# Convolution and gated feed-forward on one core: the band in 32-column tiles behind one scaling, filling matmuls in two places, one step of x last

## The chip, the cores and the metric

The kernel runs on 1 core of one Trainium2 chip. The metric is device microseconds of one execution, and the median over the runs is compared. A core has a matrix engine (TensorE, PE in the profile; its weight loads are PEld), VectorE (DVE), ScalarE (ACT), GpSimd (POOL) and SyncE (SP), which here only issues transfers. Each engine works through its own instructions in order, and they wait for each other by semaphores. Matmuls write to PSUM, and DVE or ACT copies from there to SBUF.

## The reference

A causal convolution over 7 positions, whose 8 heads of 24 channels each have their own softmax weights, followed by a gated feed-forward block:

```python
# x (8, 4096, 192), weight (8, 7)
w = softmax(weight, axis=-1)                      # per head
x_pad = concat([zeros(8, 6, 192), x], axis=1)
conv[b, s, h*24 + g] = sum_k w[h, k] * x_pad[b, s + k, h*24 + g]
t = conv.reshape(32768, 192)
out = (maximum(t @ w_gate, 0) * (t @ w_val)) @ w_out   # 192 -> 1536 -> 192
```

## The kernel before

The 32768 tokens are worked in 16 units of 2 x 1024 tokens (two streams, batches b and b + 4), each unit in two windows of 512. For a window, `gate_val` (L621) multiplies the convolved x, kept with 64 channels of each of two streams on the partitions, by 12 slices of the gate and value weights; ACT applies the relu (L632), DVE multiplies (L633), and `project_turn` (L643) multiplies by the output weights. For most of the run the convolution for later units is done beside this by ACT, DVE and POOL.

The first window has nothing to work beside, so its convolution is done by TensorE, in a prologue with this order:

1. Seven matmuls on constants (L193, `hold`, by the counts in `WARM`, in units of 128 columns) keep TensorE occupied. They write to the first bank of a PSUM tile called `held`. Four stand ahead of the spreading matmul (L203), which copies the 8 x 7 weights to 128 partitions as soon as their transfer lands, and three behind it.
2. DVE and ACT make the softmax (L275 to L295). Three DVE instructions (L299) scale the 22-wide row of weights and mask it by head, for heads 0 to 2, 3 to 5 and 6 to 7. The result is `blocks`, 128 x 8 x 22.
3. Three matmuls with zeros (L209) clear three PSUM areas. The third area is the second bank of `held`. Then 8 matmuls for each area (L335) place `blocks` along a diagonal, 16 rows at a time, so that a 118 x 112 band matrix stands there for each head. DVE casts the three areas to f16, `bands` (L343).
4. `conv_steps` (L391) multiplies x by the bands. The window is cut into 5 steps of up to 106 positions and the 192 channels into 3 groups c of 64. A step of a group is 8 matmuls, four at a time in four column tiles. Group 0 needs the first band only, group 1 also the second, group 2 the second and third. x comes from f32 rows that ACT casts step by step (L119) in the order `STEPS0 = [1, 0, 2, 3, 4]`; step 4 has its own transfer, which lands last. The order is: group 0 steps 1, 0, 2; group 1 steps 1, 0; group 0 steps 3, 4; group 1 steps 2, 3, 4; then group 2.
5. `evict` (L402) casts each group from PSUM to the f16 tile `dense[0]`, 512 columns at once: group 0 on ACT, 1 on DVE, 2 on ACT. DVE also copies the first slices of the gate and value weights to the upper partitions (`both_halves`, L231).
6. The first gate and value matmuls (L621) go by groups: gate and value of group 0, then of group 1, then of group 2, four matmuls each, which run in two pairs.

The order on each engine is that in which the code is written. Semaphore waits are set by the tile framework from what each instruction reads and writes.

Of the kernel before, what the change touches and what calls it, by code (L numbers as in the profile page):

```python
# [15 lines left out]
def kernel(  # L16
# [27 lines left out]
    STEPS = [6, 5, 2]  # L44
    TAPS = [(6, 5), (4, 3), (2, 1, 0)]
    GSUB = 5
    WARM = [(4, 4, 4, 1), (4, 4, 1)]
    STEPS0 = [1, 0, 2, 3, 4]
    CONV1 = 10


# [242 lines left out]
    nc.vector.tensor_reduce(out=blk[:, 0, :], in_=prod[:], axis=mybir.AxisListType.X, op=ALU.add)  # L294
    nc.vector.reciprocal(sm[:], sm[:])  # L295
    blocks = const.tile([128, H, BW], F16)
    for heads in BANDS:
        n = len(heads)
        nc.vector.scalar_tensor_tensor(  # L299
            out=blocks[:, heads[0] : heads[0] + n, :],  # L300
            in0=blk[:].to_broadcast([128, n, BW]),
            scalar=sm[:],
            in1=mask[:, heads[0] : heads[0] + n, :].to_broadcast([128, n, BW]),
            op0=ALU.mult,
            op1=ALU.mult,
        )
    wn = const.tile([128, KW], FP)
    nc.gpsimd.tensor_scalar(
        out=wn[:], in0=e[:, 0:KW], scalar1=sm[:], scalar2=None, op0=ALU.mult
# [18 lines left out]
    for part, heads, to, copy in zip(  # L328
        raised, BANDS, bands, [nc.vector.tensor_copy] * 3
    ):  # L330
        n = len(heads)
        for j in range(128 // HR):
            s0 = HR * j - PAD
            lo, hi = max(0, -s0), min(BW, SUB - s0)
            nc.tensor.matmul(  # L335
                out=part[:, 0 : SUB * n].rearrange("p (h t) -> p h t", t=SUB)[:, :, s0 + lo : s0 + hi],
                lhsT=Z[:, 112 - HR * j : 240 - HR * j],
                rhs=blocks[:, heads[0] : heads[0] + n, lo:hi],
                start=False,
                stop=(j == 128 // HR - 1),  # L340
                skip_group_check=True,
            )
        copy(out=to[:].rearrange("p h t -> p (h t)"), in_=part[:, 0 : SUB * n])  # L343

    tap = const.tile([128, NCH, KW], FP)

# [30 lines left out]
    def conv_steps(g, ps, c, steps):  # L377


        for jj in steps:  # L380
            col = STEP * jj
            n = min(STEP, WIN - col)
            rows = n + PAD
            for second in range(2):
                for st in range(2):
                    for k2 in range(2):
                        k = 2 * c + k2
                        h0, h1 = 32 * k // G, (32 * k + 31) // G
                        h, m = (h0, G * h1 - 32 * k) if second else (h1, 32)
                        p0 = 64 * st + 32 * k2  # L390
                        nc.tensor.matmul(  # L391
                            out=ps[p0 : p0 + m, 0, col : col + n],
                            lhsT=xts[g][0:rows, jj, st, 32 * k : 32 * k + m],
                            rhs=band(h)[0:rows, 0:n],
                            start=True,
                            stop=True,
                            tile_position=(0, p0),
                            skip_group_check=True,
                        )

    def evict(copy, g, ps, c):
        copy(out=dense[0][:, g, c, :], in_=ps[:, 0, :])  # L402

    def conv(g):

# [301 lines left out]

    dense[0] = xcpool.tile([128, 2, NCH, WIN], F16, name="xc")
    first = [psum.tile([128, 2, 512], FP, name="ps") for _ in range(NCH)]
    for c, steps in ((0, STEPS0[:3]), (1, STEPS0[:2]), (0, STEPS0[3:]), (1, STEPS0[2:]), (2, STEPS0)):  # L710
        conv_steps(0, first[c], c, steps)
    both_halves(nc.vector.tensor_copy, 0, Wg)
    both_halves(nc.vector.tensor_copy, 0, Wv)
    for c, copy in enumerate((nc.scalar.copy, nc.vector.tensor_copy, nc.scalar.copy)):
        evict(copy, 0, first[c], c)
    both_halves(nc.vector.tensor_copy, 1, Wg)
    both_halves(nc.vector.tensor_copy, 1, Wv)
    xts[2] = load_x(2)
# [82 lines left out]
```

## Time and profile before

| | |
|---|---|
| median of 3 runs (lowest, highest) | 761.65 us (761.57, 763.04) |
| span of the profiled execution, first to last instruction | 760.2 us |
| median less span | 1.45 us |
| TensorE busy | 756.0 us, 99% of the span |
| spreading matmul (L203) starts | 2.76 us |
| first band matmul (L335) starts | 4.97 us |
| first convolution matmul (L391) starts | 6.12 us |
| first gate matmul on groups 0, 1, 2 (L621) starts | 7.81, 8.24, 8.70 us |
| last matmul starts | 757.0 us |

Times within an execution are microseconds from the start of its span. A row of the timeline gives start, length, engine, line of the kernel, operation, tile written <- tile read, shape and count; in brackets stand the idle time of the engine just before it and what ended that. Rows of equal instructions are merged, so the length of a merged row reaches from the first start to the last end. Ends of matmuls are modelled.

### The profile page before, as it was taken

The page shows a single profiled execution, that of the slowest core. Times are in us where ns is not written, and L with a number is a line of the kernel's source. Part 1 is how long each engine was busy: PE and PEld are TensorE (multiplying, and loading weights), DVE is VectorE, ACT ScalarE, POOL GpSimd, SP SyncE. Part 2 cuts the span into 40 slices and gives each one's busy share as a digit, 9 for nine tenths or more (in the row PEclk, how much of TensorE's full clock was granted, in tenths as well). Part 3 has the DMA queues.
Part 4 walks back from the last instruction along what each step waited for, and adds up shares of the span by engine and source line. Part 5 has one row for each costly group of instructions (what it writes and reads, how often), then busy time and mean ns, then how long its engine had stood idle before and what let it go on. Part 6 is the DMA issues. An engine that isn't in the chain of part 4 may idle for free.

```text
span 760.2 us, 30531 instructions
## 1 busy us (share of the span) xinstructions
PE 756.0 (99%) x13724; PEld 454.8 (60%) x13724; DVE 675.8 (89%) x647; ACT 610.1 (80%) x680; POOL 461.3 (61%) x311
## 2 busy tenths in 40 slices
PE   9999999999999999999999999999999999999998
PEld 5555555565565666656666565666656556566658
DVE  7889989998998989989999899998999989897891
ACT  7897887878878788887877878788797887877671
POOL 8729649195591946829377392874919659193600
PEclk9999999999999999999999999999999999999999
DMA  8953532345324443333434324352243531240302
GB/s 142 137 69 92 79 85 46 43 96 75 85 44 52 97 66 85 55 61 83 60 85 71 66 67 55 85 85 69 56 49 93 77 86 44 23 100 9 85 2 85
DMA packets 153714, 54.07 MB, mean 71 GB/s; under 512 B 148912, under 2 KB 153584, under 8 KB 153584
## 3 DMA queue, kind: packets, MB, share of 16 engines
q1 hardware_dynamic: 117376, 37.78, 21.6%
q0 software_dynamic: 35808, 14.07, 16.4%
q8 instruction: 107, 1.75, 1.0%
q10 hardware_dynamic: 400, 0.27, 0.1%
q14 instruction: 23, 0.19, 0.1%
HBM read 28.98 MB, written 25.17 MB: 71 GB/s over the span
## 4 chain that ended last, share of the span: by engine, by line
PE 99%; DMA 0%; ACT 0%; issue 0%
PE ps L621 65%; PE ps L643 31%; PE ps L686 2%; PE ps L391 0%; DMA w<-in_weight_dram 0%; PE ps L193 0%; PE ps L335 0%; PE ps L414 0%; PE ps L209 0%; PE ps L203 0%; ACT out_s L697 0%; ACT L127 0%
## 5 line engine op out<-in xcount | busy, mean ns | idle before, releaser
L633 DVE TENSOR_TENSOR hT<-gr,ps 128x1024 f16<-128x1024 f16 (+1 forms) x385 | 469.1, 1219 | 35.5 <-ACT gr L632 8.7
L632 ACT ACTIVATE gr<-ps 128x1024 f16<-128x1024 f32 (+1 forms) x385 | 392.8, 1021 | 114.4 <-PE ps L621 114.4
L550 POOL TENSOR_TENSOR prod<-prod,prod 128x896 f32<-128x896 f32 x145 | 302.6, 2087 | 251.8 <-DVE prod L584 242.7
L621 PE MATMUL ps<-xc,Wg 64*64 64x512 f16 (+1 forms) x4464 | 318.4, 376 | 0.0
L621 PE MATMUL ps<-xc,Wv 64*64 64x512 f16 (+1 forms) x4464 | 318.3, 376 | 0.0
L643 PE MATMUL ps<-hT,Wo 64*64 64x512 f16 x4320 | 235.8, 376 | 0.0
L621 PEld LDWEIGHTS <-Wv 64*64 64x64 f16 (+1 forms) x4464 | 149.9, 106 | 98.5 <-DVE hT L633 0.3
L621 PEld LDWEIGHTS <-Wg 64*64 64x64 f16 (+1 forms) x4464 | 145.4, 107 | 103.4 <-issue 0.2
L643 PEld LDWEIGHTS <-Wo 64*64 64x64 f16 x4320 | 137.3, 107 | 95.7
L538 ACT ACTIVATE prod<-x_r,tap 128x1024 f32<-128x1024 f16 (+2 forms) x195 | 182.7, 1017 | 0.0
L574 DVE SCALAR_TENSOR_TENSOR acc<-x_r,tap,acc 128x1024 f32<-128x1024 f16 (+3 forms) x150 | 118.0, 854 | 0.0
L661 DVE STREAM_TRANSPOSE out_s<-ps 128x1024 f32<-128x1024 f32 x45 | 56.2, 1248 | 28.4 <-PE ps L643 24.4
L550 POOL TENSOR_TENSOR xc<-prod,prod 128x896 f16<-128x896 f32 x29 | 60.6, 2089 | 2.3
L479 POOL COPY x_p<-x_e 128x1536 f16<-128x1536 f16 (+1 forms) x32 | 42.2, 1351 | 0.0
L251 POOL DMA_DIRECT2D x_e<-in_x_dram x30 | 26.6, 890 | 0.0
L574 DVE SCALAR_TENSOR_TENSOR xc<-x_r,tap,acc 128x1024 f16<-128x1024 f16 (+3 forms) x30 | 25.2, 840 | 0.0
L563 ACT ACTIVATE acc<-x_r,tap 128x1024 f32<-128x1024 f16 (+3 forms) x30 | 22.5, 800 | 0.0
L656 ACT COPY turned_by<-ps 128x2 f32<-128x2 f32 x45 | 7.0, 155 | 16.8 <-PE ps L643 14.8
L686 PEld LDWEIGHTS <-hT 128*128 128x128 f16 x192 | 15.8, 98 | 0.4 <-issue 0.4
L686 PE MATMUL ps<-Wo,hT 128*128 128x192 f16 x192 | 16.0, 246 | 0.0
L697 ACT COPY out_s<-ps 128x768 f32<-128x768 f32 (+2 forms) x5 | 3.2, 638 | 12.7 <-PE ps L686 12.7
L697 DVE COPY out_s<-ps 128x192 f32<-128x192 f32 x1 | 0.4, 359 | 13.3 <-PE ps L686 13.3
(61 smaller groups left out, 74.4 us busy)
## 6 DMA issues: line engine op xcount, KB each, us to landing
out_dram<-out_s SPq DMA_DIRECT2D x125, 192.0 KB
x_e<-in_x_dram POOLq DMA_DIRECT2D x28, 384.0 KB, 6.3
x_r<-x_p SPq DMA_TRANSPOSE x116
prod<-in_moe_w_out_dram POOLq DMA_DIRECT2D x1, 576.0 KB, 8.7
prod<-in_x_dram SPq DMA_DIRECT2D x3, 168.0 KB
out_dram<-out_s SPq DMA_DIRECT2D x5, 96.0 KB
out_s<-in_x_dram POOLq DMA_DIRECT2D x2, 210.0 KB, 6.2
out_s<-in_x_dram POOLq DMA_DIRECT2D x2, 192.0 KB, 6.1
```

Of the source, the lines that this page charges most:

```text
L251: nc.gpsimd.dma_start(out=xe[:, 0:n, st, :, :].rearrange("p j c r -> p j (c r)"), in_=bass.AP(tensor=x.tensor, offset=x.offset + row * D, ...
L479: nc.gpsimd.tensor_copy(out=xp[:, js, :, st, :], in_=xe[:, js, st, :, :])
L538: nc.scalar.activation(out=both(prods[b, k], b, at, n), in_=shifted(b, c, k, t, n), func=ACTF.Copy, scale=tap[:, c, k : k + 1],)
L550: nc.gpsimd.tensor_tensor(out=acc if k < KW - 1 else xcs[b][:, w, :, :].rearrange("p c t -> p (c t)")[:, LDVE : NCH * WIN], in0=acc, in1=p ...
L563: nc.scalar.activation(out=both(accs[b], b, at, n), in_=shifted(b, c, 0, t, n), func=ACTF.Copy, scale=tap[:, c, 0:1],)
L574: nc.vector.scalar_tensor_tensor(out=result(b, at, n) if k == KW - 1 else both(acc, b, at, n), in0=shifted(b, c, k, t, n), scalar=tap[:, c ...
L621: nc.tensor.matmul(out=pss[i][q : q + M, st, :], lhsT=W[64 * st : 64 * st + 64, c, 128 * f + q : 128 * f + q + M], rhs=xcb[64 * st : 64 * ...
L632: nc.scalar.activation(out=gr[:, sts], in_=pss[0][:, sts], func=ACTF.Relu)
L633: nc.vector.tensor_tensor(out=h[:, f, sts], in0=gr[:, sts], in1=pss[1][:, sts], op=ALU.mult)
L643: nc.tensor.matmul(out=ps[64 * st : 64 * st + 64, b, :], lhsT=Wo[64 * r : 64 * r + 64, f, p, :], rhs=hs[b][64 * r : 64 * r + 64, f, st, :] ...
L661: nc.vector.transpose(out=o[:].rearrange("p t (b d) -> p b t d", b=2)[:, :, :, 32 * p : 32 * p + 32], in_=ps[:].rearrange("p b (t c) -> p ...
L686: nc.tensor.matmul(out=ps[:, i // 2, D * (i % 2) : D * (i % 2) + D], lhsT=h[:, f, st, 128 * q : 128 * (q + 1)], rhs=Wo[:, f, :, :].rearran ...
```

## The change

- The burst ahead of the spreading matmul is 4, 4, 4, 3 units of 128 columns instead of 4, 4, 4, 1.
- `blocks` is made by one DVE instruction over all 8 heads instead of three.
- The band matmuls write 32 partitions instead of 128, each in a column tile of its own (`tile_position=(0, q)`), in the order `PLACED`, so that four neighbours in the order have four different tiles.
- Two filling matmuls of 512 and 256 columns (`hold(*WARM[2])`) stand between the band and the first convolution. They write to the first bank of `held`, whose second bank held the third area of the band.
- The convolution's order is group 0 steps 1, 0, 2, 3; group 1 the same; then step 4 of group 0 and of group 1; then group 2.
- Groups 0 and 1 are copied out in two pieces: columns 0 to 317 (steps 0 to 2) and 318 to 511 (steps 3 and 4). Group 0's first piece is on DVE, ahead of the copies of the weights, and its second on ACT; group 1's first is on ACT and its second on DVE.

```diff
-    WARM = [(4, 4, 4, 1), (4, 4, 1)]
+    WARM = [(4, 4, 4, 3), (4, 4, 1), (4, 2)]
     STEPS0 = [1, 0, 2, 3, 4]
+    PLACED = [0, 2, 4, 6, 1, 3, 5, 7]
...
-    for heads in BANDS:
-        n = len(heads)
-        nc.vector.scalar_tensor_tensor(
-            out=blocks[:, heads[0] : heads[0] + n, :],
-            in0=blk[:].to_broadcast([128, n, BW]),
-            scalar=sm[:],
-            in1=mask[:, heads[0] : heads[0] + n, :].to_broadcast([128, n, BW]),
-            op0=ALU.mult,
-            op1=ALU.mult,
-        )
+    nc.vector.scalar_tensor_tensor(
+        out=blocks[:],
+        in0=blk[:].to_broadcast([128, H, BW]),
+        scalar=sm[:],
+        in1=mask[:].to_broadcast([128, H, BW]),
+        op0=ALU.mult,
+        op1=ALU.mult,
+    )
...
-        for j in range(128 // HR):
+        for j in PLACED:
+            q = HR * j // 32 * 32
             s0 = HR * j - PAD
             lo, hi = max(0, -s0), min(BW, SUB - s0)
             nc.tensor.matmul(
-                out=part[:, 0 : SUB * n].rearrange("p (h t) -> p h t", t=SUB)[:, :, s0 + lo : s0 + hi],
-                lhsT=Z[:, 112 - HR * j : 240 - HR * j],
+                out=part[q : q + 32, 0 : SUB * n].rearrange("p (h t) -> p h t", t=SUB)[
+                    :, :, s0 + lo : s0 + hi
+                ],
+                lhsT=Z[:, 112 - HR * j + q : 144 - HR * j + q],
                 rhs=blocks[:, heads[0] : heads[0] + n, lo:hi],
                 start=False,
-                stop=(j == 128 // HR - 1),
+                stop=(j % 2 == 1),
+                tile_position=(0, q),
                 skip_group_check=True,
             )
         copy(out=to[:].rearrange("p h t -> p (h t)"), in_=part[:, 0 : SUB * n])
+    hold(*WARM[2])
...
-    def evict(copy, g, ps, c):
-        copy(out=dense[0][:, g, c, :], in_=ps[:, 0, :])
+    def evict(copy, g, ps, c, cols=slice(0, WIN)):
+        copy(out=dense[0][:, g, c, cols], in_=ps[:, 0, cols])
...
-    for c, steps in ((0, STEPS0[:3]), (1, STEPS0[:2]), (0, STEPS0[3:]), (1, STEPS0[2:]), (2, STEPS0)):
+    for c, steps in ((0, STEPS0[:4]), (1, STEPS0[:4]), (0, STEPS0[4:]), (1, STEPS0[4:]), (2, STEPS0)):
         conv_steps(0, first[c], c, steps)
+    early_cols, late_cols = slice(0, 3 * STEP), slice(3 * STEP, WIN)
+    evict(nc.vector.tensor_copy, 0, first[0], 0, early_cols)
     both_halves(nc.vector.tensor_copy, 0, Wg)
     both_halves(nc.vector.tensor_copy, 0, Wv)
-    for c, copy in enumerate((nc.scalar.copy, nc.vector.tensor_copy, nc.scalar.copy)):
-        evict(copy, 0, first[c], c)
+    evict(nc.scalar.copy, 0, first[0], 0, late_cols)
+    evict(nc.scalar.copy, 0, first[1], 1, early_cols)
+    evict(nc.vector.tensor_copy, 0, first[1], 1, late_cols)
+    evict(nc.scalar.copy, 0, first[2], 2)
```

Where this puts the instructions is shown at two places, with the semaphores that each instruction waits for (DVE_49 counts what DVE has finished, PE_49 what TensorE, Activation_49 what ACT). The line numbers of the changed kernel are a few higher: L193 became L194, L343 L346, L391 L395, L402 L406 and L621 L625.

The first place is TensorE between the band matmuls and the convolution. Before, with the first matmul of each channel group (`band_188`, `band_189` and `band_190` are the first, second and third band; x is in `out_s`):

```order
L335 MATMUL ps<-blocks,Z 128x2x6
L391 LDWEIGHTS out_s [waits Activation_49]
L391 MATMUL ps<-band_188,out_s 32x106 [waits DVE_49]
...
L391 MATMUL ps<-band_189,out_s 32x106 [waits DVE_49]
...
L391 MATMUL ps<-band_190,out_s 32x106 [waits DVE_49]
```

The same place now; the three bands are `band_186`, `band_187` and `band_188`:

```order
L335 MATMUL ps<-blocks,Z 32x2x6
L194 LDWEIGHTS const-bfloat16-1.0
L194 MATMUL ps<-const-bfloat16-1.0 128x512 [waits DVE_49]
L194 LDWEIGHTS const-bfloat16-1.0
L194 MATMUL ps<-const-bfloat16-1.0 128x256
L395 LDWEIGHTS out_s [waits Activation_49]
L395 MATMUL ps<-band_186,out_s 32x106
...
L395 MATMUL ps<-band_187,out_s 32x106 [waits PE_49]
...
L395 MATMUL ps<-band_188,out_s 32x106 [waits PE_49]
```

The waits of the three first readers for DVE, which casts the bands, are gone. The first filling matmul, ahead of them all, has the only wait for DVE.

The second place is where the groups are copied out (`xc` is the tile `dense[0]`). Before, on ACT and then on DVE from the third band cast on:

```order
L119 CAST out_s<-prod_90 96x384 [waits DMAHW4_49]
L402 CAST xc<-ps 128x512 [waits PE_49] x2
...
L343 CAST band_190<-ps 128x224 [waits PE_49]
L231 COPY Wg<-Wg 64x3x128 [waits DMASW0_49]
L231 COPY Wv<-Wv 64x3x128 [waits DMASW1_49]
L402 CAST xc<-ps 128x512 [waits PE_49]
```

The same now, ACT first:

```order
L120 CAST out_s<-prod_90 96x384 [waits DMAHW4_49]
L406 CAST xc<-ps 128x194 [waits DVE_49]
L406 CAST xc<-ps 128x318 [waits PE_49]
L406 CAST xc<-ps 128x512 [waits PE_49]
...
L346 CAST band_188<-ps 128x224 [waits PE_49]
L406 CAST xc<-ps 128x318 [waits PE_49]
L232 COPY Wg<-Wg 64x3x128 [waits DMASW0_49]
L232 COPY Wv<-Wv 64x3x128 [waits DMASW1_49]
L406 CAST xc<-ps 128x194 [waits Activation_49]
```

ACT's piece of group 0 waits for DVE and no longer for TensorE, and DVE's piece of group 1 waits for ACT. The copies of the two weight slices now stand behind DVE's piece of group 0.

## The prediction

> **What bounds the kernel now.** I read the page first: its first part and the shares of the chain that ended last.
>
> ```profile
> span 760.2 us, 30531 instructions
> PE 756.0 (99%) x13724; PEld 454.8 (60%) x13724; DVE 675.8 (89%) x647; ACT 610.1 (80%) x680; POOL 461.3 (61%) x311
> PE ps L621 65%; PE ps L643 31%; PE ps L686 2%; PE ps L391 0%; DMA w<-in_weight_dram 0%; PE ps L193 0%; PE ps L335 0%; PE ps L414 0%; PE ps L209 0%; PE ps L203 0%; ACT out_s L697 0%; ACT L127 0%
> ```
>
> TensorE (PE) is busy for 99% of the span and is the chain itself. From the gate and value matmuls (L621) on, nothing else holds it, so whatever moves their start moves the end by as much. The change lies wholly ahead of them. So I read the chain of waits for the first 12 us (start, length, what):
>
> ```profile
> 0.87 1.75 DMA w<-in_weight_dram
> 2.76 0.56 PE ps L203 x2
> 3.32 1.07 PE ps L193 x3
> 4.39 0.75 PE ps L209 x3
> 5.14 1.05 PE ps L335 x24
> 6.19 1.61 PE ps L391 x120
> 7.81 4.33 PE ps L621 x37
> ```
>
> This chain says PE throughout, but pieces of PE here are themselves held by VectorE (DVE) and ScalarE (ACT). The timeline of the same stretch shows by whom (start, length, engine, line; the last columns are the idle time before and its releaser):
>
> ```profile
> 4.06 1.78 ACT L119 CAST out_s<-prod 112x384 f16<-112x384 f32 x4
> 4.63 0.67 DVE L299 SCALAR_TENSOR_TENSOR blocks<-blk,sm,mask 128x66 f16<-128x66 f32 x3
> 4.97 1.22 PE L335 MATMUL ps<-blocks,Z 128*128 128x48 f16 x24
> 5.56 0.51 DVE L343 CAST band<-ps 128x336 f16<-128x336 f32 x1 [0.26 <-PE ps L335]
> 5.56 1.22 DVE L343 CAST band<-ps 128x336 f16<-128x336 f32 x3 [0.26 <-PE ps L335]
> 5.99 0.50 DVE L343 CAST band<-ps 128x336 f16<-128x336 f32 x1
> 6.12 1.68 PE L391 MATMUL ps<-band,out_s 112*32 112x106 f16 x120
> 6.18 0.51 ACT L119 CAST out_s<-prod 96x384 f16<-96x384 f32 x1 [0.34 <-DMA prod<-in_x_dram]
> 7.17 0.58 ACT L402 CAST xc<-ps 128x512 f16<-128x512 f32 x1 [0.48 <-PE ps L391]
> 7.81 0.39 PE L621 MATMUL ps<-xc,Wg 64*128 64x512 f16 x2
> 8.06 0.58 ACT L402 CAST xc<-ps 128x512 f16<-128x512 f32 x1 [0.30 <-PE ps L391]
> 8.24 0.40 PE L621 MATMUL ps<-xc,Wg 64*128 64x512 f16 x2
> 8.45 0.40 PE L621 MATMUL ps<-xc,Wv 64*128 64x512 f16 x2
> 8.70 0.39 PE L621 MATMUL ps<-xc,Wg 64*128 64x512 f16 x2
> ```
>
> The convolution starts at 6.12, 0.05 after the first band cast ends (5.56 + 0.51 = 6.07). The first gate matmul starts at 7.81, 0.05 after channel group 0 is copied out (7.17 + 0.58). Groups 1 and 2 are first read at 8.24 and 8.70, which are the marks to beat. A hand-over from one engine to another costs about 0.05.
>
> Two paces of PE follow. The 24 band matmuls stream 154 columns for each of 8 heads, 1232 in 1.05 us: 0.85 ns a column. A pair of 512 columns takes 8.45 - 8.24 = 0.21: 0.41 ns a column. The convolution is already at the fast pace: its second group can start at 5.99 + 0.50 + 0.05 = 6.54, and its last 96 matmuls, 24 rounds of four, start by 6.12 + 1.68 - 0.21 = 7.59 (0.21 is the length of one, quoted below), 0.045 a round, or 0.42 a column. So PE doubles its pace at about 6.1, after 2.8 us of work without a pause since 3.32.
>
> **The change part by part.** Durations for the new shapes come from these groups (count, busy, mean ns):
>
> ```profile
> L391 PE MATMUL ps<-band,out_s 112*32 112x106 f16 x48 | 1.6, 212 | 0.0
> L574 DVE SCALAR_TENSOR_TENSOR acc<-x_r,tap,acc 128x1024 f32<-128x1024 f16 x70 | 89.1, 1272 | 0.0
> L574 DVE SCALAR_TENSOR_TENSOR acc<-x_r,tap,acc 128x256 f32<-128x256 f16 x70 | 33.6, 479 | 0.0
> L299 DVE SCALAR_TENSOR_TENSOR blocks<-blk,sm,mask 128x66 f16<-128x66 f32 x2 | 0.5, 292 | 0.0
> L343 DVE CAST band<-ps 128x336 f16<-128x336 f32 x2 | 0.9, 502 | 0.3 <-PE ps L335 0.3
> L697 DVE COPY out_s<-ps 128x192 f32<-128x192 f32 x1 | 0.4, 359 | 13.3 <-PE ps L686 13.3
> L697 ACT COPY out_s<-ps 128x384 f32<-128x384 f32 x1 | 0.5, 478 | 1.2 <-PE ps L686 1.2
> L697 ACT COPY out_s<-ps 128x192 f32<-128x192 f32 x1 | 0.3, 318 | 1.5 <-PE ps L686 1.5
> ```
>
> *Filling ahead of the spreading matmul.* 256 columns more, 0.22 us at 0.85. The burst it joins is over long before the weight lands (0.87 + 1.75 = 2.62). Cost: nothing; without that cover, 0.22.
>
> *One scaling of all heads.* The first of three pieces took 0.29 and let the band start at 4.97. One piece of 176 columns takes 0.292 + 110 x 1.03 ns (slope of the L574 rows) = 0.41 and ends at 5.04; the band starts at 5.09, 0.12 later.
>
> *Band in 32-column tiles.* No row shows such a tile at the slow pace. The nearest is the convolution, in which four column tiles run at once. Two rounds of 66 columns cost 0.11 for each set of heads, where eight matmuls of 462 columns in all took 0.39. From the first matmul to the first cast was 5.56 - 4.97 = 0.59, so 0.20 of it is not streaming; now 0.31, and the first cast starts at 5.40. If the tiles did not overlap it would stay 0.59: 5.68. I take 5.40. The three casts still follow each other on DVE for 1.22, so the third ends at 6.62 instead of 6.78 (bound 6.90).
>
> *Filling matmuls ahead of the convolution.* Here the rows of the order decide. Before, the first reader of each band waited for DVE by itself; now none does, and the first filling matmul has the only wait for DVE between band and convolution. It must therefore stand for all three casts. PE works in order, so the convolution, which used to start after the first cast, now stands behind the third: the filling starts at 6.62 + 0.05 = 6.67. Its 768 columns cost 0.32 at the fast pace and 0.65 at the slow one. I take the slow one: the pace changed after 2.8 us of unbroken work, and now PE has stood still from about 5.4 to 6.67, so the filling is the first work after a pause. For the convolution I take the fast pace, the only one that it shows. Call its start P = 7.32 (6.99 with fast filling). Loss so far 1.20.
>
> *Step 4 of x last, and the split copies.* Nothing is left to gain from the order of steps: the cast of step 4 is over at 6.18 + 0.51 = 6.69, before P. Group 0 is finished after 64 + 8 matmuls, 18 rounds, P + 0.81. Before, it was finished 8 rounds after 6.54, at 6.90, and read at 7.17, so 0.28 lies between. DVE starts the early piece at P + 1.09. It cannot start sooner: the ACT piece of step 4 waits for DVE alone, so DVE's piece must already stand behind step 4. The early piece, 318 columns, takes 0.48 (502 less 18 x 1.0); ACT's late piece starts 0.04 after its end and takes 0.32; the first gate matmul follows at P + 1.09 + 0.48 + 0.04 + 0.32 + 0.05 = P + 1.98. One copy of 0.58 has become two in a row. The copies of Wg and Wv stand behind the early piece on DVE, and at 0.4 and 0.3 us they are done by P + 2.1, beside ACT's piece.
>
> Group 1: ACT goes on about 0.08 before its last piece ends (four casts of 0.505 in 1.78), takes 318 columns in 0.42 (318 + 126 x 0.83, slope of the ACT rows) until P + 2.27; DVE's piece waits for ACT, 0.04 + 0.36, so PE reads group 1 at P + 2.72. Group 2: ACT follows at P + 2.2 and is done at P + 2.8, ahead of its reader 0.43 after group 1 (two pairs). Nothing to pay there; before, 0.46 lay between, so 0.03 comes back.
>
> **Sum.** Group 1 is read at 7.32 + 2.72 = 10.04 against 8.24: 1.80 later, less 0.03: **+1.77 us** on the profiled span of 760.2. What lies around the span (761.65 - 760.2 = 1.45) I leave as it is, so the median 761.65 becomes **763.4**. Nothing later gives it back: PE is full from there on.
>
> **The rivals.** *Fast filling* (0.23): PE is at its fast pace at 6.67, P = 6.99, +1.44, 763.1. For it: PE is as busy from 3.32 to 5.4 as before. Against it: the pause.
>
> *Slow convolution* (0.20): the pause keeps PE slow until group 0 is done; 18 rounds of 106 x 0.85 = 0.09 instead of 0.045 add 0.81, +2.58, 764.2. For it: a burst with a pause behind it, the one up to 3.32, did not bring the fast pace. Against it: no slow row of the convolution. [...]
>
> *Only one of the two waits costs* (0.11): filling free of the third cast, copies in a row: P = 6.06, group 1 at 8.78, +0.51; or filling held, pieces side by side: group 0 at P + 0.81 + 0.28 + 0.32 + 0.05 = 8.78, group 2 at P + 2.43 = 9.75 (conv's end P + 1.35, 0.44 to ACT as now, 0.58, 0.05), +1.05. Between 762.2 and 762.7.
>
> *The change does what it says* (0.06), not slower: the filling waits for the first band at most and lies in the time of its cast, from the band's end at 5.41 to 6.06 (slow pace); the pieces leave as steps end. P = 6.06, group 2 at P + 2.43 = 8.49 against 8.70: -0.21, 761.4. It holds if the third cast ends after the filling starts; the order speaks against it.
>
> **How the numbers follow.** The forecast has 0.40. About 0.2% (1.52 us, 763.17) is what a measurement of this kernel can tell from no change. Slower by more: most of the forecast (0.34), a little under half of fast filling (0.11), all of slow convolution (0.20): 0.65. Within: the rest of these, both cases of one wait, and most of the last: 0.32. Faster: 0.03, since the whole head before 7.81 offers no such gain. The range 762.6 to 764.6 holds the forecast, fast filling, most of the slow convolution and a part of the one-wait case; 0.3 either way around 763.4 is the likeliest's own.
>
> **What would show it.** In the new timeline: the first band cast at about 5.4 and the third's end near 6.6; PE idle from 5.4 to 6.7; the filling (L194) starting only behind the third cast (L346), two matmuls over 0.65 or 0.32; the convolution (L395) as one block from about 7.3; on ACT the piece of 194 columns starting only when DVE's 318 end; the first gate matmul (L625) at 9.3, group 1 at 10.0. Wrong if the filling starts before 6, if DVE's early piece starts before step 4 is done, or if the convolution runs in rounds of 0.09.

## The result, and the profile after

The changed kernel is slower: a median of 764.77 us (763.48 to 768.26, 7 runs) against 762.53 us (761.57 to 763.04, 7 runs) for the kernel before, a ratio of 1.0037 with a 95% interval of 1.0022 to 1.0051. That is 0.17 above the forecast's range and 1.4 above its time. The spread grew too: 1.5 us before, 4.8 now.

The execution that was profiled is the quickest of the seven (763.48, span 761.8), and has to be read as such. Its page, first part and the first line of the shares of the chain that ended last:

```profile
span 761.8 us, 30535 instructions
...
PE 756.0 (99%) x13726; PEld 425.8 (56%) x13726; DVE 677.1 (89%) x646; ACT 610.8 (80%) x681; POOL 461.3 (61%) x311
...
PE 99%; DVE 1%; ACT 0%; issue 0%
```

TensorE has as much to do as before (756.0), and the span is 1.6 longer. New in the chain is 1% of DVE. The chain of waits shows where it stands (start, length, what; its rows from 4.89 on):

```profile
4.89 0.27 PE ps L335 x8
5.18 1.23 DVE band L346 x3
6.46 0.49 PE ps L194 x2
6.94 1.08 PE ps L395 x80
8.05 0.49 DVE xc L406
8.57 0.55 DVE Wg L232
9.11 0.46 DVE Wv L232
9.62 4.47 PE ps L625 x36
```

Before, the chain was PE alone from 2.76 on. Now it leaves TensorE twice in these rows: for the three band casts in a row, and for DVE's early piece with two weight copies behind it. (Ahead of them, from 3.14 to 4.89, it runs through the softmax and the scaling on DVE and ACT.) The timeline of the same stretch (start, length, engine, line, operation; last the idle time before and its releaser):

```profile
4.43 0.40 DVE L298 SCALAR_TENSOR_TENSOR blocks<-blk,sm,mask 128x176 f16<-128x176 f32 x1
...
4.89 0.35 PE L335 MATMUL ps<-blocks,Z 128*32 128x48 f16 x24
5.18 1.22 DVE L346 CAST band<-ps 128x336 f16<-128x336 f32 x3 [0.35 <-PE ps L335]
...
6.46 0.49 PE L194 MATMUL ps<-const-bfloat16-1.0 128*128 128x512 bf16 x2 [1.22 <-DVE band L346]
...
6.87 1.57 PE L395 MATMUL ps<-band,out_s 112*32 112x106 f16 x120
...
8.05 0.49 DVE L406 CAST xc<-ps 128x318 f16<-128x318 f32 x1 [1.64 <-PE ps L395]
...
8.47 0.50 POOL L232 COPY Wg<-Wg 64x384 f16<-64x384 f16 x1
8.57 0.55 DVE L232 COPY Wg<-Wg 64x384 f16<-64x384 f16 x1
...
8.94 0.62 PE L625 MATMUL ps<-xc,Wg 64*128 64x512 f16 x2 [0.50 <-ACT xc L406]
9.04 0.52 DVE L232 COPY Wv<-Wv 64x384 f16<-64x384 f16 x1
...
9.59 0.36 DVE L406 CAST xc<-ps 128x194 f16<-128x194 f32 x1
...
9.99 0.91 DVE L232 COPY Wg<-Wg 64x384 f16<-64x384 f16 x1
10.01 0.39 PE L625 MATMUL ps<-xc,Wg 64*128 64x512 f16 x2
...
10.44 0.40 PE L625 MATMUL ps<-xc,Wg 64*128 64x512 f16 x2
...
10.87 0.38 PE L625 MATMUL ps<-xc,Wg 64*128 64x512 f16 x1
```

The 24 band matmuls are done in 0.35 instead of 1.22 (0.48 at the slow pace, in the next profile), and most of what they won is lost at once: TensorE then stands still for 1.22, until the third cast is done and the filling can start. Groups 0, 1 and 2 are read at 8.94, 10.01 and 10.44, against 7.81, 8.24 and 8.70. The last group is 1.74 later, as forecast, in an execution that is not the typical one.

The changed kernel run again (`again`, median 765.2) was profiled in an execution of 765.07, close to its median. Its timeline, TensorE alone:

```profile
4.89 0.48 PE L335 MATMUL ps<-blocks,Z 128*32 128x48 f16 x24
6.51 0.80 PE L194 MATMUL ps<-const-bfloat16-1.0 128*128 128x512 bf16 x2 [1.14 <-DVE band L346]
7.24 2.75 PE L395 MATMUL ps<-band,out_s 112*32 112x106 f16 x120
9.94 0.61 PE L625 MATMUL ps<-xc,Wg 64*128 64x512 f16 x2
...
10.74 0.66 PE L625 MATMUL ps<-xc,Wg 64*128 64x512 f16 x2
...
11.60 0.66 PE L625 MATMUL ps<-xc,Wg 64*128 64x512 f16 x2
12.02 0.61 PE L625 MATMUL ps<-xc,Wv 64*128 64x512 f16 x2
12.45 0.83 PE L625 MATMUL ps<-xc,Wg 64*128 64x512 f16 x6
```

Same program, same order, and all of it at half the pace until 12.45: the convolution in 2.75 instead of 1.57, the gate pairs 0.43 apart instead of 0.22. The row at 12.45 is the seventh pair. Before, the seventh pair stood at 9.13:

```profile
8.91 0.39 PE L621 MATMUL ps<-xc,Wv 64*128 64x512 f16 x2
9.13 0.83 PE L621 MATMUL ps<-xc,Wg 64*128 64x512 f16 x6
```

So 12.45 - 9.13 = 3.32 is lost by the seventh pair, against 3.1 in the span (763.3 - 760.2). In the quick execution the seventh pair stands at 10.87, 1.74 later than before. The other 1.58 comes with the slow pace, in the same order of instructions, and it is the difference of the two times (765.07 - 763.48 = 1.59).

### The profile page after: what moved, and what is told of

Same layout as the page of the kernel before. It is cut to its first block, busy times and chain, and to the rows that moved or that the text cites. A ratio compares the mean times of both kernels' runs of the same rounds, so it can differ in the third digit from the quotient of the medians.

```text
span 761.8 us, 30535 instructions
## 1 busy us (share of the span) xinstructions
PE 756.0 (99%) x13726; PEld 425.8 (56%) x13726; DVE 677.1 (89%) x646; ACT 610.8 (80%) x681; POOL 461.3 (61%) x311
## 4 chain that ended last, share of the span: by engine, by line
PE 99%; DVE 1%; ACT 0%; issue 0%
PE ps L625 65%; PE ps L647 31%; PE ps L690 2%; PE ps L395 0%; PE ps L194 0%; DVE band L346 0%; PE ps L418 0%; DVE Wg L232 0%; PE ps L204 0%; DVE xc L406 0%; DVE Wv L232 0%; DVE blocks L298 0%; DVE prod L288 0%; ACT out_s L701 0%; DVE blk L295 0%
## 5 line engine op out<-in xcount | busy, mean ns | idle before, releaser
L625 PE MATMUL ps<-xc,Wg 64*64 64x512 f16 (+1 forms) x4464 | 314.8, 376 | 0.5 <-ACT xc L406 0.5
L625 PE MATMUL ps<-xc,Wv 64*64 64x512 f16 (+1 forms) x4464 | 314.9, 376 | 0.1
L625 PEld LDWEIGHTS <-Wv 64*64 64x64 f16 (+1 forms) x4464 | 143.9, 106 | 105.0 <-DVE Wv L232 0.4
L625 PEld LDWEIGHTS <-Wg 64*64 64x64 f16 (+1 forms) x4464 | 134.4, 107 | 115.1 <-DVE Wg L232 0.9
L647 PEld LDWEIGHTS <-Wo 64*64 64x64 f16 x4320 | 126.3, 107 | 106.7
```

Of the source, the lines that this page charges most:

```text
L625: nc.tensor.matmul(out=pss[i][q : q + M, st, :], lhsT=W[64 * st : 64 * st + 64, c, 128 * f + q : 128 * f + q + M], rhs=xcb[64 * st : 64 * ...
L647: nc.tensor.matmul(out=ps[64 * st : 64 * st + 64, b, :], lhsT=Wo[64 * r : 64 * r + 64, f, p, :], rhs=hs[b][64 * r : 64 * r + 64, f, st, :] ...
```

## The experiments

Each kernel ran in five rounds beside the kernel before, whose median was 762.56, 762.41, 762.60 and 762.76 in the four groups. Since the distributions have long upper ends, the table has three numbers for each: the median less that of before, the lowest time, and how many executions lay above 764.2 (2 of 134 did for the kernel before). "Waits" says whether the filling stands behind the third band cast, "pieces" whether groups 0 and 1 leave in two pieces.

| kernel | waits | pieces | median less before | lowest | above 764.2 |
|---|---|---|---|---|---|
| changed kernel (the runs of the result) | yes | yes | +2.24 | 763.48 | 6 of 7 |
| again | yes | yes | +2.64 | 763.46 | 11 of 12 |
| wideband | yes | yes | +2.54 | 763.45 | 6 of 10 |
| weightsfirst | yes | yes | +2.69 | 763.22 | 5 of 7 |
| slicesfirst | yes | yes | +1.65 | 763.26 | 6 of 11 |
| wholecopy | yes | no | +2.51 | 762.67 | 4 of 6 |
| fillonly | yes | no | +0.74 | 762.43 | 5 of 12 |
| keepbusy | yes, pause filled | yes | +1.37 | 763.47 | 4 of 11 |
| keepbusy_slices | yes, pause filled | yes | +1.10 | 763.38 | 4 of 11 |
| keepbusy_whole | yes, pause filled | no | +0.56 | 762.69 | 1 of 11 |
| fillspread | no | yes | +0.94 | 762.61 | 1 of 11 |
| fillspread_whole | no | no | +0.41 | 761.96 | 2 of 11 |
| nofill | no filling | yes | +0.49 | 762.03 | 2 of 11 |
| nofill_whole | no filling | no | +0.39 | 762.10 | 0 of 11 |
| splitonly | no filling | yes | -0.06 | 762.13 | 0 of 11 |
| warmonly | no filling | no | -0.05 | 761.87 | 0 of 11 |
| poolslice | no filling | no | -0.22 | 761.90 | 0 of 11 |

None of these kernels leaves out a part of the computation: the filling matmuls compute nothing that the output needs.

### The wait of the filling

**again**: the changed kernel, nothing edited.

> The changed kernel unaltered, for a second profile in another phase of the clock. In the first profile TensorE was at its fast pace already at 4.9 us (band matmuls), the span was 761.8, and the run was the fastest of seven (763.48, median 764.77). Theory 'pause': in the slower executions TensorE is at the slow pace for some part of 5 to 11 us, and this profile, if its span is 763 or more, shows filling matmuls 0.43 apart, convolution rounds of 0.09 or gate pairs of 0.43 there. Rival 'elsewhere': the slower executions lose their 1 to 2 us after 11 us, and the first 11 us look like the first profile's.

Measured: 765.2 (763.46 to 769.85), ratio 1.0039 (1.0026 to 1.0053). The profile is shown above. The forecast's time is that of its quickest executions, and its typical one is slow through the convolution and the first gate pairs.

**nofill** takes the two filling matmuls away:

```diff
-    hold(*WARM[2])
```

> Leaves out only the two filling matmuls ahead of the convolution. Theory 'wait': the convolution starts 0.05 after the first band cast, at about 5.74 instead of 6.87, group 1 is read at about 8.45 (10.01 in the changed kernel, 8.24 before), and the median comes back to within 0.5 us of the kernel before. Rival 'copies': the loss lies in the copies in two pieces; the median stays 1.5 us or more above the kernel before.

Measured: 763.05, ratio 1.0008 (0.9999 to 1.0016). Its timeline, TensorE alone:

```profile
5.13 0.48 PE L335 MATMUL ps<-blocks,Z 128*32 128x48 f16 x24
6.05 1.80 PE L394 MATMUL ps<-band,out_s 112*32 112x106 f16 x120 [0.43 <-DVE band L346]
8.30 0.39 PE L624 MATMUL ps<-xc,Wg 64*128 64x512 f16 x2 [0.45 <-ACT xc L405]
```

The convolution stands behind the first cast alone again, 0.43 after the band. Without the two matmuls 2.15 of the 2.64 are gone, so the median came out as the theory of the wait had it. The marks inside did not: the convolution starts at 6.05 (expected 5.74), group 1 is read at 9.02 (expected 8.45).

**fillspread** keeps both matmuls and lets them write to a bank that no cast reads:

```diff
-                out=held[:, 0, 0 : 128 * reps],
+                out=(held[:, 0, :] if at is None else at)[:, 0 : 128 * reps],
...
-    hold(*WARM[2])
+    hold(*WARM[2], at=spread[:, 1, :])
```

> The same two filling matmuls, written to the second bank of the PSUM tile of the spreading matmul, which DVE and ACT have long read. Theory 'wait': it is the wait for the third cast that costs, not the 768 columns; the filling runs at about 5.1, the convolution starts at 5.4 to 5.8, and the median is that of the kernel without filling, to 0.4 us. Rival 'columns': the filling itself is on the path and the median stays 0.6 us or more above the kernel without filling.

Measured: 763.5, ratio 1.0006 (0.9998 to 1.0015). So the wait, with what follows from it, costs 1.7 (765.2 - 763.5). The columns of the filling cost 0.45 by the medians (763.5 - 763.05), between the two expectations, and nothing by the ratios (1.0006 here, 1.0008 in nofill), so a price for them is not shown. What makes the wait is the tile `held` that filling and third area share: the two are in different banks and never overlap.

### The pause and the pace

**keepbusy** keeps the wait and gives TensorE 1536 more columns, which wait for nothing, ahead of the filling that waits:

```diff
+    hold(4, 4, 4, at=spread[:, 1, :])
     hold(*WARM[2])
```

> The changed kernel with three more filling matmuls of 512 columns, written to the spreading matmul's tile, between the band and the filling that waits: TensorE works through most of its pause of 1.4 us, and the convolution still starts behind the third cast. Theory 'pause': the pause makes TensorE fall back to or stay at the slow pace in most executions, so the median falls from 764.8 to about 763.5 and the spread of the runs narrows to about 1 us. Rival 'phase': the spread comes from when the clock rises at all, whatever TensorE does; median and spread stay as in the changed kernel.

Measured: 763.93, ratio 1.0021 (1.0009 to 1.0032). The pause shrinks from 1.14 to 0.45, the convolution starts at 6.87 as in the changed kernel's quick profile, and the median falls by 1.27 although TensorE was given more to do. Work without a purpose made the kernel faster, so about half of the loss in the median goes with the pause and not with the wait itself. The spread did not narrow to 1 us as expected: the times reach from 763.47 to 768.36, and four of 11 still lay above 764.2.

**fillonly** is the kernel before with the waiting filling alone:

```diff
-    WARM = [(4, 4, 4, 1), (4, 4, 1)]
+    WARM = [(4, 4, 4, 1), (4, 4, 1), (4, 2)]
...
+    hold(*WARM[2])
```

> The kernel before with nothing but the two filling matmuls of 512 and 256 columns ahead of the convolution, in the tile of the third band. Theory 'wait': the filling starts 0.05 after the third cast, near 6.83, the convolution at 7.15 (fast pace) or 7.48 (slow) instead of 6.12; the median is 1.0 to 1.7 us above the kernel before. The band takes 1.05 here, so TensorE's pause is 0.8 and not 1.4, and the slowest runs should stay below those of the changed kernel. Rival: filling between band and convolution is hidden, median within 0.4 us.

Measured: 763.34, ratio 1.0016 (1.0007 to 1.0025): 0.74 above the kernel before, under the 1.0 to 1.7 expected. Behind the old, long band the pause is 0.64 in the profile, and five of 12 executions lay above 764.2.

**wideband** is the changed kernel with the band in 128 columns, one matmul after the other, as before:

```diff
-                out=part[q : q + 32, 0 : SUB * n].rearrange("p (h t) -> p h t", t=SUB)[
+                out=part[:, 0 : SUB * n].rearrange("p (h t) -> p h t", t=SUB)[
...
-                lhsT=Z[:, 112 - HR * j + q : 144 - HR * j + q],
+                lhsT=Z[:, 112 - HR * j : 240 - HR * j],
...
-                tile_position=(0, q),
```

> The changed kernel with one part undone: the band matmuls write all 128 columns again, one after the other, about 1.05 us instead of 0.35, all else as changed. TensorE's pause ahead of the filling becomes about 0.65 instead of 1.2 to 1.4. Theory A (the length of the pause decides when the fast pace comes): the median falls though TensorE has more to do, to 763.3 to 764.2, and the profile shows the convolution at 1.6 us. Rival (the pause's length does not matter, the wait and the two pieces set the time): median 765.2 to 765.5.

Measured: 765.3, ratio 1.0033 (1.0018 to 1.0047): the rival's number, and the expectation from the length of the pause missed. The profile happened on one of the quick executions (763.47), TensorE alone:

```profile
4.89 1.12 PE L335 MATMUL ps<-blocks,Z 128*128 128x48 f16 x24
6.74 0.49 PE L194 MATMUL ps<-const-bfloat16-1.0 128*128 128x512 bf16 x2 [0.73 <-DVE band L345]
7.16 1.56 PE L394 MATMUL ps<-band,out_s 112*32 112x106 f16 x120
9.15 0.39 PE L624 MATMUL ps<-xc,Wg 64*128 64x512 f16 x2 [0.43 <-ACT xc L405]
```

A pause of 0.73 is thus no cure. The times fall into two heaps, four at 763.45 to 763.82 and six from 765.23 up, so the median only says on which side the middle fell: the changed kernel had 2 of its 19 in the lower heap, this one 4 of 10, which may be chance.

The heaps and the pause can be set beside the trace's record of when TensorE had its full clock. Its start, from the start of the span, for 16 profiled executions, and the pause between band and filling (or convolution) in each. Two, splitonly and fillspread_whole, had no such record; their gate pairs close up to 0.22 apart at about 9.4, without a pause in either:

```
kernel           full clock from   pause
after                 4.40          1.22
wideband              5.66          0.73
fillonly              5.79          0.64
weightsfirst          9.48          1.14
slicesfirst          10.01          1.14
wholecopy            11.31          1.14
again                12.46          1.14

keepbusy              4.74          0.45
before                6.08          none
nofill                6.64          0.43
keepbusy_slices       7.17          none
warmonly              7.38          none
fillspread            7.46          none
poolslice             8.48          none
nofill_whole          9.48          0.43
keepbusy_whole        9.60          none
```

The record is 757.76 us long in `after`, 754.35 in the kernel before and 750.93 in `again`, and each of the 16 has one of these three lengths, 3.41 us apart. With no pause, or one of up to 0.45, the full clock came at any time from 4.7 to 9.6. With a pause of 0.64 or more it came by 5.8, no later than the pause began (5.2 to 6.0), or at 9.48 and later; never in between, where six of the other nine lie. What sets these moments no run shows.

The pause alone does not tell early from late. In nofill and in nofill_whole it is 0.43, and the full clock came at 6.64 in the one and at 9.48 in the other. In keepbusy_whole there is no such pause, and it came at 9.60. TensorE's wait for the weight's transfer, ahead of the spreading matmul, does not tell the first two apart either: 0.20 in nofill and 0.19 in nofill_whole; it is 0.46 in keepbusy_whole, and 0.36 in the kernel before, which had its full clock at 6.08. That is the reading of 16 profiles; how much idle time puts the full clock off was not measured by itself.

### The two pieces

**wholecopy** is the changed kernel with whole-group copies as before, and **nofill_whole** has no filling besides (its diff is both):

```diff
-    evict(nc.vector.tensor_copy, 0, first[0], 0, early_cols)
...
-    evict(nc.scalar.copy, 0, first[0], 0, late_cols)
-    evict(nc.scalar.copy, 0, first[1], 1, early_cols)
-    evict(nc.vector.tensor_copy, 0, first[1], 1, late_cols)
-    evict(nc.scalar.copy, 0, first[2], 2)
+    for c, copy in enumerate((nc.scalar.copy, nc.vector.tensor_copy, nc.scalar.copy)):
+        evict(copy, 0, first[c], c)
```

> The changed kernel with the copies of before: whole groups of 512 columns, the weight copies first on DVE; filling, band tiles, one scaling and the order of steps stay. Theory 'copies in a row': the first gate matmul follows the convolution's start by about 1.75 instead of 2.07 and group 2 by 2.6 instead of 3.57 (fast pace), so the fastest runs fall from 763.5 to about 762.5; the wait and the pause stay, so the median stays about 1.5 us above the kernel before. Rival: TensorE's wait for the third cast is the whole of the loss and the copies make under 0.3 us.

Measured: 764.92 (6 runs), ratio 1.0026 (1.0012 to 1.0041). The median hardly moved, where 1.5 above the kernel before was expected, but the lowest time fell from 763.46 to 762.67. By these, the pieces cost 0.8 where the pace comes early. The quick profiles bear it out: fillonly, with whole copies, reads group 2 at 9.28, 2.43 after its convolution's start, `after` 3.57 after it. Where the pace comes late (this profile: convolution 2.75) the whole copy and the pieces both lie beside the slow convolution.

> The changed kernel without the two filling matmuls and with the copies of before: what is left is the longer first burst, one scaling, band tiles and the order of steps. If wait and copies are the whole loss, this is at or below the kernel before: convolution start near 5.8 to 6.05, group 2 read 2.6 later at 8.4 to 8.65 against 8.70; the median 0 to 0.4 us below before. If the band tiles or the order cost something of their own, it stays above.

Measured: 762.8, ratio 1.0005 (0.9996 to 1.0014), 0.25 under nofill; the lowest times are alike (762.10 and 762.03). The expectation of 0 to 0.4 below the kernel before missed: by the median it lies 0.39 above, though the interval leaves room for no difference. Whether band tiles, single scaling or the order of steps cost something of their own is thus open. The profile has a slow convolution (2.75).

**splitonly** is the kernel before with the two pieces and nothing else:

```diff
-        copy(out=dense[0][:, g, c, :], in_=ps[:, 0, :])
+        copy(out=dense[0][:, g, c, cols], in_=ps[:, 0, cols])
...
+    evict(nc.vector.tensor_copy, 0, first[0], 0, early_cols)
...
+    evict(nc.scalar.copy, 0, first[0], 0, late_cols)
+    evict(nc.scalar.copy, 0, first[1], 1, early_cols)
+    evict(nc.vector.tensor_copy, 0, first[1], 1, late_cols)
+    evict(nc.scalar.copy, 0, first[2], 2)
```

> The kernel before with nothing but the copies in two pieces, in the changed order on DVE and ACT. Where the convolution runs at the fast pace, group 2 is read about 3.4 after its start instead of 2.58 (8.70 less 6.12), 0.7 to 0.9 us later. Where it runs at the slow pace, its 2.7 us hide the copies and nothing is lost. The median is 0.3 to 0.8 us above the kernel before. Rival 'copies are hidden always': within 0.2 us.

Measured: 762.54, ratio 0.9998 (0.9989 to 1.0007): no cost, and the expected price missed. In its profile the convolution runs at the slow pace, and DVE's weight copies take 0.27 to 0.30. Behind the late start of the changed kernel they take 0.55 and 0.52 (rows of the result) and hold the value matmuls and group 1's late piece, which makes the pieces dearer there. That is not all of their price: in nofill's profile, with the first copies at 0.29 and 0.32 and the full clock from 6.64, group 2 is still read 3.40 after the convolution's start (9.45 - 6.05), against 2.58 before. No quick execution of splitonly was profiled, and why its median shows nothing stays open.

**fillspread_whole** (fillspread with whole copies) and **keepbusy_whole** (keepbusy with whole copies) close the square.

> As the last, with the two filling matmuls written to the spreading matmul's tile, free of the casts. Theory 'pause': it has no pause of TensorE over 0.3 us between 3 us and the convolution, so its slowest runs are below those of the kernel without filling; its fastest are 0 to 0.5 us above them, since 0.65 of filling at the slow pace ends near 6.1. Rival: filling brings nothing, and it is slower in all runs by the columns alone.

> The changed kernel with the copies of before and three more filling matmuls that are free of the casts: wait for the third cast kept, pause of TensorE filled, copies not in a row. Theory 'pause': compared with the same kernel without the three (764.9 median, 762.7 to 765.8), the fastest stay at about 762.5 and the median falls to 763 to 763.5, since the fast pace comes before the convolution in most runs. Rival 'phase': median about 764.5 again.

Measured: 762.82, ratio 1.0010 (1.0001 to 1.0019), and 763.16, ratio 1.0011 (1.0002 to 1.0019). Each is 0.7 to 0.8 under its partner with pieces (763.5 and 763.93). The second met its expectation: against wholecopy's 764.92, the filled pause took 1.76 off. The first missed one part: with no pause its slowest executions should have stayed below those of nofill_whole (763.31), and two of 11 reached 764.83 and 765.35. So late executions occur without this pause too.

**warmonly** is the kernel before with the longer first burst, 4, 4, 4, 3:

> The kernel before with only the longer first burst (4, 4, 4, 3). If its 256 columns are hidden behind the weight's transfer, the median is that of the kernel before to 0.2 us; if more work before 2.4 us makes the fast pace come earlier, 0.2 to 0.5 us below it; if the weight often lands before the burst is over, 0.1 to 0.2 us above.

Measured: 762.55, ratio 0.9999 (0.9990 to 1.0007). It is free, as forecast.

### The weight copies on DVE

The profile of keepbusy_whole fell on its slowest execution (765.78), and shows a cost that no theory had. Its timeline, all engines:

```profile
10.22 0.52 POOL L232 COPY Wg<-Wg 64x384 f16<-64x384 f16 x1
...
10.51 2.60 DVE L232 COPY Wg<-Wg 64x384 f16<-64x384 f16 x1
10.67 0.52 POOL L232 COPY Wv<-Wv 64x384 f16<-64x384 f16 x1
...
11.12 0.51 POOL L232 COPY Wg<-Wg 64x384 f16<-64x384 f16 x1
...
12.47 0.50 POOL L232 COPY Wv<-Wv 64x384 f16<-64x384 f16 x1
...
13.17 0.82 PE L626 MATMUL ps<-xc,Wg 64*128 64x512 f16 x5 [1.22 <-DVE Wg L232]
```

(POOL's rows at 11.57 and 12.02 are left out; they are like the others.) A copy of slice 1 that takes 0.28 in keepbusy and fillonly started 0.29 after POOL had begun on a row of six copies, and ended 0.14 after the last of them (13.11 against 12.97). TensorE stood 1.22 for it. In the quick profile of the changed kernel the same copy starts at 9.99 and takes 0.91.

**weightsfirst** puts DVE's copies of slice 0 ahead of the early piece, **slicesfirst** those of slices 0 and 1 (the diff is that of slicesfirst):

```diff
+    for s in range(2):
+        both_halves(nc.vector.tensor_copy, s, Wg)
+        both_halves(nc.vector.tensor_copy, s, Wv)
     evict(nc.vector.tensor_copy, 0, first[0], 0, early_cols)
-    both_halves(nc.vector.tensor_copy, 0, Wg)
-    both_halves(nc.vector.tensor_copy, 0, Wv)
...
-    both_halves(nc.vector.tensor_copy, 1, Wg)
-    both_halves(nc.vector.tensor_copy, 1, Wv)
```

> The changed kernel with the two weight copies ahead of the early piece of group 0 on DVE; the copies in two pieces stay. If the queue on DVE behind the early piece is what held the second gate matmul and group 1 (weight copies of 0.55 and 0.52 at 8.6 to 9.6 in the first profile, 0.39 and 0.32 before), gate and value of group 0 run without a gap and group 2 is read about 3.2 after the convolution's start instead of 3.57, 0.3 to 0.4 us off the fastest runs. If the pieces that wait for each other are all of it, nothing changes.

Measured: 765.1, ratio 1.0033 (1.0022 to 1.0044). It changes nothing that the median shows; the profile has the late pace again.

> The changed kernel, with DVE's copies of weight slices 0 and 1 (eight of about 0.28 us) ahead of the early piece of group 0, so that none of them is left on DVE when POOL starts its six copies in a row at about 10.2. Theory A (most of the distance of the changed kernel from the kernel before is TensorE's fast pace coming late, the DVE copies blocked beside POOL make only the executions above 766.5): median 764.9 to 765.6, none of the executions above 766.5, the profile shows the convolution in 2.75 us. Theory B (blocked weight copies make a part of the typical time too): median 763.8 to 764.7. In both, an execution with the fast pace from the start pays about 0.3 to 0.8 for the early piece, which stands behind eight copies.

Measured: 764.41 (763.26 to 765.4), ratio 1.0021 (1.0012 to 1.0029). This is in the interval of B. Against its own kernel before it is 1.0 nearer than again was, but six of 11 are still above 764.2, and the profile (TensorE alone) has the late pace:

```profile
6.51 0.80 PE L194 MATMUL ps<-const-bfloat16-1.0 128*128 128x512 bf16 x2 [1.14 <-DVE band L346]
7.24 2.75 PE L395 MATMUL ps<-band,out_s 112*32 112x106 f16 x120
9.94 0.40 PE L625 MATMUL ps<-xc,Wg 64*128 64x512 f16 x2
...
10.66 0.39 PE L625 MATMUL ps<-xc,Wg 64*128 64x512 f16 x2
```

**keepbusy_slices** is keepbusy with slicesfirst:

> The changed kernel with both suspected costs taken away: 1536 columns of filling that wait for nothing stand ahead of the filling that waits, so that TensorE has no pause, and DVE copies weight slices 0 and 1 ahead of the early piece. Keepbusy alone had a median of 763.93 and one execution at 768.36. Theory A: median 763.7 to 764.4 with the fast pace by 7 us in the profile, none above 766.5. If the high executions are of another origin, one or two above 766.5 remain.

Measured: 763.86 (763.38 to 764.82), ratio 1.0017 (1.0008 to 1.0026), hardly under keepbusy's 763.93, without its execution at 768.36. So with the pause filled, the early copies take nothing from the typical time, as A had it. Above 766.5 lay 6 of 64 executions of the seven kernels that keep the wait and DVE's late slice 1 copies and have more than the filling (the changed kernel both times, wideband, weightsfirst, wholecopy, keepbusy, keepbusy_whole; 7 + 12 + 10 + 7 + 6 + 11 + 11), and none of the 22 of slicesfirst and keepbusy_slices. By chance alone that happens about one time in six, so that these copies make the executions from 766 to 770 is possible but not shown.

The record has a second candidate. Four of the six (768.26, 768.36, 768.6 and 768.75) have a mean granted clock of 0.998, which only one other execution has (fillspread_whole's 765.35); all others that list a clock have 0.999 or 1.0. Over 768 us, 0.998 is an estimated 2.3 to 3.8 us at half clock (0.5, the low value in the records of `before` and `after`). The falling of the clock at the program's end makes at most 0.92 us of that in the profiles kept. So by this estimate the four had the low clock for some 1.4 us or more besides; where, is not shown, since no trace of one was kept.

**poolslice** is the kernel before with DVE's slice 1 copies given to POOL:

```diff
+    pool_halves(1)
...
-    both_halves(nc.vector.tensor_copy, 1, Wg)
-    both_halves(nc.vector.tensor_copy, 1, Wv)
```

> The kernel before with the copies of weight slice 1 given from DVE to POOL, ahead of POOL's slice 2, so that DVE has four copies fewer when TensorE begins on the gate. If DVE's copies beside POOL's cost the kernel before something: 762.2 to 762.5 against 762.55. If not, or if slice 2 now comes late: 762.5 to 763.5.

Measured: 762.54 against 762.76, ratio 0.9998 (0.9989 to 1.0006). No difference can be told, and no version measured beats the kernel before.

## Why the prediction was wrong

The direction was right, and the reason for it. The time was that of a case which the kernel reaches in about one execution of ten, and met there by luck. The steps, in microseconds (`after` is the quick execution, `again` the typical one; P is the convolution's start):

| step | forecast | after | again |
|---|---|---|---|
| third band cast ends | 6.62 | 6.41 | 6.47 |
| filling starts behind it | 6.67 | 6.46 | 6.51 |
| filling to convolution | 0.65 | 0.41 | 0.73 |
| P | 7.32 | 6.87 | 7.24 |
| group 0 read | P + 1.98 | P + 2.07 | P + 2.70 |
| group 1 read | P + 2.72 | P + 3.14 | P + 3.50 |
| group 2, behind group 1 | 0.43 | 0.43 | 0.86 |
| span against before | +1.77 | +1.6 | +3.1 |

- *The wait.* Right in every part: the filling starts 0.05 behind the third cast, TensorE stands for 1.1 to 1.2, and the convolution's 120 matmuls are one block. nofill and fillspread show that the wait with its consequences is worth 1.7 of the 2.64.
- *The step that failed* is the sentence "For the convolution I take the fast pace, the only one that it shows", beside filling at the slow pace. It let TensorE change its pace between filling and convolution, in one execution that had the fast pace early, and took that row for a property of the convolution. The profiled execution of before had the pace from 6.08; splitonly, whose TensorE does the same up to there, ran its convolution in 2.75. The pause was named as a reason for slow filling, and its effect was ended 0.65 later without a reason. In its place the runs showed the convolution in 2.75 instead of 1.57 and gate pairs 0.43 apart until 12.45: 1.58 us more than the quick execution, in rounds of 0.09 (2.75 over 30), the sign that the prediction had named for being wrong. The four profiles with a pause of 1.14 all have the slow convolution (2.58 to 2.75), 17 of the changed kernel's 19 executions lie above the quick two, and filling the pause (keepbusy) takes 1.27 of the loss away.
- *The slow convolution* was the rival with 0.20, at 764.2, and is, by these profiles, what most executions do. Its group 1 was due at 7.32 + 2.72 + 0.81 = 10.85, and `again` has 10.74. It was too short by the rest: it let the slow pace end with group 0, and the four pairs from group 1 to the seventh took 1.71 instead of 0.89 (12.45 - 10.74, 9.13 - 8.24), 0.82 more. With that it comes to 765.0, within 0.2 of both medians. In all, the slow pace costs 1.58 in `again` (12.45 - 10.87, the seventh pair), where the sum of this rival took 0.81.
- *Slow or fast filling.* Both occur, 0.73 and 0.41, with the pace.
- *The two pieces.* The order of events was as forecast (DVE's piece, ACT's behind it), and P + 2.07 is near P + 1.98. Mis-sized was "at 0.4 and 0.3 us they are done by P + 2.1, beside ACT's piece" for the weight copies: in `after` they took 0.55 and 0.52 beside POOL's and ended at P + 2.69, which put group 1's late piece at 9.59 instead of 9.18 (the forecast's P + 2.31), 0.41 of the 0.42 by which group 1 missed its forecast. By the lowest times the pieces cost 0.8 behind the wait (wholecopy against again, keepbusy_whole against keepbusy).
- *Why the quick execution hits 763.4 all the same*: two misses cancel. Casts and filling were 0.45 quicker than forecast, and group 1 was 0.42 slower behind them.
- *Scaling, burst, order of steps.* One scaling took 0.40 (forecast 0.41); the burst is free (warmonly); the order of steps was not measured by itself, and had nothing to win with step 4's cast long over. The band's first matmul came 0.08 earlier than before instead of 0.12 later, because the scaling began 0.20 earlier in this execution (4.43 against 4.63); the band to its first cast took 0.29 here and 0.35 in `again`, at the slow pace that the forecast's 0.31 assumed.

What stays open: how much of the 766 to 770 us executions is DVE's long copies beside POOL's and how much the lower granted clock, and why slicesfirst is lower in the median by 0.8 while keepbusy_slices is not lower than keepbusy. Not tried: a `held` tile cut into two tiles of one bank each, so that the waits fall back to what each reader needs with filling in its place; fillspread stands nearest to it.

## What to carry to other kernels

Before work is put "into a gap" of an engine that runs in order, look at which wait moves to it: two banks of one tile count as one here, and a filler inherited the latest wait of three. Speeding up the producer ahead of such a wait mostly lengthens the pause: 0.64 off the band (0.48 in `again`, 1.12 in wideband) brought the filling 0.23 forward and made the pause 0.41 longer. And a pause near the start can be followed by half pace for long: behind the one that ended at 6.51 in `again`, the full pace came at 12.46. Read a profile of the start as one draw: set its pace beside the spread of the runs before a row is taken for a property of the code.

## What the runs showed of the hardware

- A DVE copy of 0.28 us (64 x 384, f16) took 0.55, 0.91 and 2.60 us beside POOL copies of 0.50 to 0.53 (`after` and keepbusy_whole): in the 2.60 it ended only 0.14 after a row of six POOL copies. What makes it long no run shows by itself.
- The moment of TensorE's full pace varied from 4.4 to 12.5 us after the start, and the lengths of its record are 3.41 apart. With a pause of 1.14 us between 5.2 and 6.8 it came at 9.48 to 12.46 (four profiles); with a pause of 0.43 it came at 9.48 in nofill_whole and at 6.64 in nofill.
